# Loading the first quarter of W1 with two DMAs and two waits

## Chip, cores, metric

One NeuronCore of a Trainium2 chip. The metric is device microseconds of one execution, median of several. One execution in each set is profiled; times inside the profile are microseconds from the start of the span, which is about 1.7 us shorter than the device time. Engines: PE is TensorE (PEld its weight loads), DVE VectorE, ACT ScalarE, POOL GpSimd, SP SyncE; ACTq and SPq are their sequencers, which issue DMAs.

## The reference

```python
# x: (1, 2048, 640) bf16; w1: (640, 1536); w2: (1536, 640); wqkv: (640, 1920); wo: (640, 640)
xn = _layernorm(x)
return x + linear_attention(xn, wqkv, wo) + (gelu(xn @ w1 + b1) @ w2 + b2)
```

All that matters here is the first product, `xn @ w1`: it can start when the first 128 rows of x are normalised and transposed, and the first columns of W1 are in SBUF.

## The kernel before

A small planner records instructions for each engine and puts a semaphore wait on an instruction for every resource (`r_...`) that it reads or writes and that another engine or a DMA last wrote. Each DMA has a semaphore of its own. W1 lies in SBUF as `W1[p, k, f]`, row `128*k + p`, and is loaded in four quarters of 384 columns. The loads, in order of issue on each engine:

```python
        FW = F // NW1
        def dma_w1(i, eng="sync"):
            dma_w(eng, W1[:, :, i * FW:(i + 1) * FW], w1v[:, :, i * FW:(i + 1) * FW], r_W1[i])
        dma_x(0, 1)
        dma_w("scalar", b1tmp[:], B_b1.rearrange("(a p) -> a p", p=P), r_b1tmp)
        dma_w1(0, "scalar")
        dma_x(1, 1)
        dma_w1(1)
        dma_x(2, 1)
        dma_w1(2)
        # ... x tile 3, quarter 3, the rest of x, all on SyncE
```

I call the quarters 0 to 3 in code "quarter 1" to "quarter 4" in the text; the change touches quarter 1. The first three blocks of hidden units, for the first 128 rows of x, are computed in two parts, since the transposed x tile 0 comes in two pieces:

```python
        def h_first(jbs):
            bs = [take(1) for _ in jbs]
            for (ks, res) in (((0, 1), r_xnTA), ((2, 3, 4), r_xnT[0])):
                for jb, b in zip(jbs, bs):
                    Pl.ins("tensor", [(lambda e, k=k, jb=jb, b=b: e.matmul(
                        bank(b, 0, P), W1[:, k, jb * P:(jb + 1) * P], xnT[:, k, 0:P],
                        start=(k == 0), stop=(k == DT - 1))) for k in ks],
                        reads=[r_W1[jb * P // FW], res], writes=[B_[b]])
        # ... then one GELU for each block on ScalarE

        filler(10)                         # matmuls on zeros, to raise TensorE's clock
        ln_stats(0)                        # layer norm statistics of x tile 0
        ln_half(1, 0); ln_half(1, 1); ln_aggr(1)
        norm0(0, CA, r_xnA)                # columns 0 to 255 of x tile 0
        norm0(CA, D, r_xnB)                # the rest
        dA, sA, bA = transp0(0, 2, r_xnA)  # TensorE
        filler(1)
        dB, sB, bB = transp0(2, DT, r_xnB)
        # VectorE copies the first piece to xnT (r_xnTA), ScalarE the second (r_xnT[0])
        # ...
        b1_step()                          # transposes b1 on TensorE
        ln_norm(1)
        h_first([0, 1, 2])
```

The "first part" below is 6 matmuls over rows 0 to 255 of W1, the "second part" 9 matmuls over the other 384.

## Time and profile before

| | before |
|---|---|
| device time, median of 3 (range) | 210.89 us (210.71 to 210.95) |
| span of the profiled execution | 209.0 us |
| TensorE busy | 204.9 us, 98% |
| share of TensorE in the chain that ended last | 92% |
| second part of the first units starts | 7.38 us |

The page of the kernel before, its busy line and its chain of work that ended last:

```profile
PE 204.9 (98%) x1599; PEld 141.0 (67%) x1599; DVE 108.8 (52%) x227; ACT 75.1 (36%) x142; POOL 20.2 (10%) x61
...
PE 92%; DVE 6%; issue 1%; DVEq 0%
```

TensorE is the bound. From 7.4 to 60 us the start times of its matmuls show no pause over 0.03 us. So a microsecond that TensorE loses before 7.4 us is lost in the total, and the place to look is the first 8 us. The timeline there, before (start, duration, engine, line, operation, out<-in, count; in brackets the idle time before it and what ended that; in all these cuts "..." or a jump in time stands for lines left out):

```profile
0.80 0.63 ACTq L234 DMA_DIRECT2D b1tmp<-in_B_b_dram  x1
0.81 0.87 SPq L230 DMA_DIRECT2D xPK<-in_A_x_dram  x2
1.46 0.41 ACTq L234 DMA_DIRECT2D W<-in_B_w_dram  x1
1.73 0.43 SPq L234 DMA_DIRECT2D W<-in_B_w_dram  x1
...
6.72 0.09 PEld L303 LDWEIGHTS ps<-ident,b1tmp 12*128 12x128 bf16 x1
...
6.83 0.49 ACT L408 ACTIVATE xnT<-ps 128x384 bf16<-128x384 bf16 x1 [3.44 <-PE ps L375]
6.84 1.22 PE L385 MATMUL ps<-xnT,W 128*128 128x128 bf16 x15
...
7.38 0.51 PEld L385 LDWEIGHTS ps<-xnT,W 128*128 128x128 bf16 x9 [0.20 <-ACT xnT L408]
```

L385 is `h_first`. Its first 6 matmuls start at 6.84, when the transpose of b1 has left TensorE; the other 9 at 7.38, released by ScalarE's copy (L408), which ran from 6.83 to 7.32. The DMA issues, before (size, median time from issue to landing):

```profile
W<-in_B_w_dram SPq DMA_DIRECT2D x3, 480.0 KB, 7.0
W<-in_B_w_dram ACTq DMA_DIRECT2D x1, 480.0 KB, 5.2
```

Quarter 1, issued by ScalarE at 1.46, lands 5.2 us later: each W1 DMA has sixteen completions in the trace, and the last of them, which I call its landing, is at 6.68. In this execution it does not hold TensorE.

### The profile page before, as it was taken

How to read it: one execution, taken by the hardware profiler on the slowest of the kernel's cores; microseconds unless marked ns; L12 is line 12 of the kernel's file. 1: busy time of each engine (PE TensorE's matmuls, PEld its weight loads, DVE VectorE, ACT ScalarE, POOL GpSimd, SP SyncE). 2: the span in 40 equal slices, each digit the busy share in tenths (PEclk: the TensorE clock that was granted, in tenths of full speed). 3: DMA queues.
4: the chain of work that ended last, by engine and by line, in shares of the span. 5: the costliest groups of instructions: out<-in, count | busy, mean ns of one | idle time of the engine just before them, and what ended most of it. 6: DMA issues, size and time to landing. Idle time of an engine off the chain costs nothing.

```text
span 209.0 us, 3950 instructions
## 1 busy us (share of the span) xinstructions
PE 204.9 (98%) x1599; PEld 141.0 (67%) x1599; DVE 108.8 (52%) x227; ACT 75.1 (36%) x142; POOL 20.2 (10%) x61
## 2 busy tenths in 40 slices
PE   7999999999999999999999999999999999999995
PEld 2799987444457777777756565577777777777775
DVE  4589970000008888999178975478633522523322
ACT  2689887666676444111253576100000000000000
POOL 3245568200000000000000000000000000000000
DMA  6999668997000000000000000591120111001001
GB/s 164 348 349 112 105 129 130 376 332 260 3 0 0 0 0 3 0 3 0 0 0 5 0 0 3 193 313 57 63 59 32 58 42 55 31 31 35 31 34 61
DMA packets 22507, 17.86 MB, mean 85 GB/s; under 512 B 9176, under 2 KB 22488, under 8 KB 22488
## 3 DMA queue, kind: packets, MB, share of 16 engines
q1 hardware_dynamic: 21808, 17.11, 29.1%
q10 hardware_dynamic: 680, 0.49, 0.9%
q8 instruction: 12, 0.20, 0.4%
q14 instruction: 7, 0.06, 0.1%
HBM read 12.62 MB, written 2.62 MB: 73 GB/s over the span
## 4 chain that ended last, share of the span: by engine, by line
PE 92%; DVE 6%; issue 1%; DVEq 0%
PE ps L617 33%; PE ps L355 25%; PE ps L487 10%; PE ps L476 10%; PE ps L509 5%; DVE PQ L466 3%; PE ps L298 2%; PE ps L653 2%; DVE ek L464 1%; DVE W L533 1%; PE ps L529 1%; PE ps L545 1%; DVE ZB L523 1%; PE ps L555 1%; PE ps L385 1%
## 5 line engine op out<-in xcount | busy, mean ns | idle before, releaser
L355 PE MATMUL ps<-xnT,W 128*128 128x128 bf16 (+2 forms) x435 | 52.0, 282 | 0.0
L617 PE MATMUL ps<-W,HG 128*128 128x320 bf16 x360 | 51.4, 299 | 0.0
L355 PEld LDWEIGHTS ps<-xnT,W 128*128 128x128 bf16 x435 | 35.6, 98 | 15.6
L617 PEld LDWEIGHTS ps<-W,HG 128*128 128x128 bf16 x360 | 35.1, 98 | 14.2 <-issue 0.4
L359 ACT ACTIVATE HG<-ps,b1c 128x128 bf16<-128x128 f32 (+2 forms) x87 | 40.1, 493 | 12.4 <-PE ps L355 10.3
L464 DVE TENSOR_SCALAR ek<-ek 128x512 bf16<-128x512 bf16 (+1 forms) x36 | 11.0, 305 | 42.7 <-ACT ek L463 41.6
L636 DVE TENSOR_TENSOR out_sb<-ps,xnT 128x640 bf16<-128x640 f32 x15 | 12.4, 825 | 36.2 <-PE ps L617 36.1
L463 ACT ACTIVATE ek<-ps 128x512 bf16<-128x512 f32 (+1 forms) x36 | 23.2, 645 | 20.4 <-PE ps L509 11.2
L617 PE MATMUL ps<-Msb,PQ 128*128 128x320 bf16 x150 | 22.5, 299 | 0.0
L509 PE MATMUL ps<-xnT,Wqkv 128*128 128x512 bf16 x100 | 22.1, 379 | 0.0
L476 PE MATMUL ps<-Wqkv,xnT 128*128 128x320 bf16 x160 | 21.9, 299 | 0.0
L487 PE MATMUL ps<-xPK,xn_tm 128*128 128x320 bf16 x160 | 21.9, 299 | 0.0
L476 PEld LDWEIGHTS ps<-Wqkv,xnT 128*128 128x128 bf16 x160 | 15.7, 98 | 6.2
L487 PEld LDWEIGHTS ps<-xPK,xn_tm 128*128 128x128 bf16 x160 | 15.7, 98 | 6.1
L617 PEld LDWEIGHTS ps<-Msb,PQ 128*128 128x128 bf16 x150 | 14.6, 98 | 5.7
L509 PEld LDWEIGHTS ps<-xnT,Wqkv 128*128 128x128 bf16 x100 | 11.6, 117 | 9.6 <-issue 0.2
L466 DVE SCALAR_TENSOR_TENSOR PQ<-ps,ek 128x512 bf16<-128x512 f32 x20 | 13.8, 692 | 2.1
L311 DVE BATCH_NORM_STATS2 stats<-xPK 128x6 f32<-128x320 bf16 x32 | 13.6, 466 | 2.3 <-DMA xPK<-in_A_x_dram 2.3
L466 DVE SCALAR_TENSOR_TENSOR xPK<-ps,ek 128x640 bf16<-128x640 f32 x16 | 13.2, 824 | 1.7
L497 DVE TENSOR_TENSOR Msb<-Msb,xPK 128x640 f32<-128x640 f32 x14 | 11.6, 825 | 0.5
L491 ACT ACTIVATE W<-ps 128x640 bf16<-128x640 f32 x5 | 3.5, 704 | 18.2 <-PE ps L487 14.6
L321 POOL TENSOR_TENSOR rstd<-aggr,mhalf 128x1 f32<-128x1 f32 x16 | 9.1, 568 | 8.9 <-DVE aggr L319 8.9
(68 smaller groups left out, 93.7 us busy)
## 6 DMA issues: line engine op xcount, KB each, us to landing
xnT<-in_A_x_dram SPq DMA_DIRECT2D x4, 640.0 KB, 6.2
Wqkv<-in_A_wqkv_dram SPq DMA_DIRECT2D x3, 800.0 KB, 6.7
out_dram<-out_sb SPq DMA_DIRECT2D x15, 160.0 KB, 1.8
W<-in_B_w_dram SPq DMA_DIRECT2D x1, 1920.0 KB, 15.3
W<-in_B_w_dram SPq DMA_DIRECT2D x3, 480.0 KB, 7.0
xPK<-in_A_x_dram SPq DMA_DIRECT2D x2, 640.0 KB, 9.5
Wo<-in_A_wo_dram SPq DMA_DIRECT2D x1, 800.0 KB, 10.5
xPK<-in_A_x_dram SPq DMA_DIRECT2D x4, 160.0 KB, 4.2
```

Of the source, the lines that this page charges most:

```text
L311: Pl.ins(v, lambda e: e.bn_stats(stats[:, s, 6 * h:6 * h + 6], x_in[:, t, h * HW:(h + 1) * HW]), reads=[r_x[t]], writes=[r_stats[s][h]])
L355: Pl.ins("tensor", [(lambda e, k=k: e.matmul(bank(b, 0, w), W1[:, k, jb * P:(jb + 1) * P], xnT[:, k, tok], start=(k == 0), stop=(k == DT - ...
L359: Pl.ins("scalar", lambda e: e.activation(HG[:, jb, tok], bank(b, 0, w), ACT.Gelu_apprx_tanh, bias=b1c[:, jb:jb + 1]), reads=[B_[b], r_b1c ...
L463: Pl.ins("scalar", lambda e: e.activation(e2, src, ACT.Exp), reads=br, writes=[r_ek[s]])
L464: Pl.ins(v, lambda e: e.tensor_scalar(et, et, 1.0, 1e-6, ALU.min, ALU.add), reads=[r_ek[s]], writes=[r_ek[s]])
L466: Pl.ins(v, lambda e: e.scalar_tensor_tensor(out=d2, in0=src, scalar=0.0, in1=e2, op0=ALU.max, op1=ALU.add), reads=br + [r_ek[s]], writes= ...
L476: fns.append(lambda e, k=k, h=h, b=b, t=t: e.matmul(bank(b + h, 0, HW), xnT[:, k, t * P:(t + 1) * P], Wqkv[:, k, D + h * HW:D + (h + 1) * ...
L487: Pl.ins("tensor", [(lambda e, t=t, h=h, b=b, f=f: e.matmul(bank(b + h, 0, HW), xn_tm[:, t, f * P:(f + 1) * P], PK[:, t, h * HW:(h + 1) * ...
L497: Pl.ins(v, lambda e, t=t: e.tensor_tensor(out=zsum, in0=zsum, in1=PK[:, t, :], op=ALU.add), reads=[r_PK[t], r_zsum], writes=[r_zsum])
L509: Pl.ins("tensor", [(lambda e, k=k, j=j, b=b: e.matmul(bank(b), Wqkv[:, k, j:D:DT], xnT[:, k, cc], start=(k == 0), stop=(k == DT - 1))) fo ...
L617: return lambda e: e.matmul(bank(b + h, 0, HW), l, r[:, h * HW:(h + 1) * HW], start=(i == 0), stop=(i == JT + DT - 1))
L636: Pl.ins(v, lambda e: e.tensor_tensor(out=halves(out_sb[:, s, :]), in0=pair(b), in1=halves(x_res[:, t, :]), op=ALU.add), reads=B_[b:b + 2] ...
```

## The change

The intent: rows 0 to 255 are all that the first part reads, so load them with a DMA of their own, and let the first part start without the other 384 rows.

```diff
+        r_W1a = R_("W1_0a")
@@
-        dma_w1(0, "scalar")
+        dma_w("scalar", W1[:, 0:2, 0:FW], w1v[:, 0:2, 0:FW], r_W1a)
+        dma_w("scalar", W1[:, 2:DT, 0:FW], w1v[:, 2:DT, 0:FW], r_W1[0])
@@ def h_first
-                        reads=[r_W1[jb * P // FW], res], writes=[B_[b]])
+                        reads=[r_W1a if res is r_xnTA else r_W1[0], res], writes=[B_[b]])
```

The order of instructions on TensorE, VectorE, GpSimd and SyncE is unchanged; ScalarE issues one DMA more.

## The prediction

> **What bounds it now.** TensorE: busy 98% of the 209.0 us span, 92% of the chain that ended last, granted clock 1.00. From 7.4 to 60 us I find no pause of TensorE over 0.03 us in the trace's start times, so what delays TensorE before 7.4 us passes into the total almost one to one.
>
> **The first microseconds (timeline, DMA issues with time to landing).** ScalarE issues b1 (0.80, taking 0.63) and the first W1 quarter at 1.46, taking 0.41; SyncE issues x tiles 0 and 1 (0.81, 1.25), then W1 quarter 2 at 1.73. Quarter 1 lands 5.2 us after issue: 6.68. Quarter 2 lands at 7.82. TensorE ends the transposes of x tile 0, does the b1 transpose at 6.73, and starts the first part of the first units (6 matmuls, rows 0 to 255) at 6.84. Its other operand was copied by 6.45, and the b1 transpose holds TensorE until about 6.83. So quarter 1 arrives some 0.15 us before it can matter. The second part (9 matmuls) starts at 7.38, released by ScalarE's copy (6.83 to 7.32), not by W1: the chain of waits names that copy, 0.20 us idle.
>
> **What the change does.** No engine instruction is added or reordered; ScalarE gets one more DMA issue (0.41 us, early; its next needed work is at 6.83). First-part matmuls wait for 192 KB, second-part ones for the other 288 KB.
> - Gain: rows 0 to 255 land earlier, an estimate of 5 to 6 us. The first part still cannot start before the b1 transpose is done, 6.8. Worth 0 to 0.1 us (up to 0.2 if in unprofiled runs quarter 1 lands later).
> - Cost: the second DMA is issued when the first's issue is over, about 1.9 us, 0.17 us *after* SyncE's quarter 2. The landings here follow the order of issue across both issuers: 6.68 (quarter 1), 7.82 (quarter 2, 480 KB, +1.14), 8.30 (x tile 2, 160 KB, +0.49), 9.79 (quarter 3, +1.49). Quarter 1 on ScalarE's queue did not share with SyncE's quarter 2 as equals, or it would not land 1.14 us ahead. The Trainium skill (DMA: Bandwidth & Descriptors, "Issuing engines are not separate DMA queues") says they share 16 engines whoever issues; its "Queues, rings and completion order" has round robin between queues. This trace looks more like order of issue. So I expect the 288 KB behind quarter 2: the bytes up to there are those of before up to quarter 2, landing about 7.8 (7.5 if they alternate). The second part then starts at about 7.85 in place of 7.38: +0.45 us, and TensorE has no later slack.
>
> **Time.** 210.89 + 0.45 x about 0.7 (the chance that order of issue holds): 211.2 us; 210.75 to 211.6 in 8 of 10. Faster by 2%: 0.01; within: 0.97; slower: 0.02.
>
> **What would show it.** Timeline: first part at 6.8 as before; first matmul of the second part at 7.8, released by a W1 DMA, not by the copy. DMA issues: the first piece lands about 4 us after issue, the second about 5.9.
>
> **What would make it wrong.** ScalarE's second piece served ahead of quarter 2 (its queue preferred, or the issue shorter): landing about 6.7, time equal, perhaps 0.1 us less. Quarter 1 arriving late in ordinary executions: then a small gain. A shift of x tile landings or of the clock's warming (fillers run at 0.43 us each, half rate, until about 6.8).

## The result

| | before | after |
|---|---|---|
| device time, median of 6 (range) | 210.87 us (210.71 to 211.03) | 211.44 us (211.03 to 212.19) |
| ratio, 95% interval | | 1.0030 (1.0013 to 1.0047) |
| span of the profiled execution | 209.0 us | 209.7 us |
| first part starts | 6.84 us | 6.57 us |
| second part starts | 7.38 us | 8.12 us |

A ratio is the mean time of one kernel's fast runs over that of the other's of the same rounds, so not quite the ratio of the medians. A run more than 1.5% above the fastest of its kernel is marked slow, and is in no ratio. The loss is 0.3%, far inside the 2% that would be called slower, but it is resolved.

The page of the kernel after, the same two lines:

```profile
PE 204.0 (97%) x1599; PEld 140.6 (67%) x1599; DVE 108.7 (52%) x227; ACT 75.0 (36%) x142; POOL 20.1 (10%) x61
...
PE 89%; DVE 6%; DMA 3%; issue 1%; ACTq 0%; DVEq 0%
```

A DMA now has 3% of the chain; there was none. The timeline after, the lines that answer to those of before:

```profile
1.46 0.92 ACTq L235 DMA_DIRECT2D W<-in_B_w_dram  x2
...
1.72 0.43 SPq L235 DMA_DIRECT2D W<-in_B_w_dram  x1
...
6.56 0.49 ACT L410 ACTIVATE xnT<-ps 128x384 bf16<-128x384 bf16 x1 [2.66 <-PE ps L377]
...
6.57 0.51 PE L387 MATMUL ps<-xnT,W 128*128 128x128 bf16 x6
...
8.12 0.50 PEld L387 LDWEIGHTS ps<-xnT,W 128*128 128x128 bf16 x9 [1.22 <-DMA W<-in_B_w_dram]
```

ScalarE's copy (L410) was done at 7.05; the second part still starts only at 8.12, released by a W1 DMA. The DMA issues after:

```profile
W<-in_B_w_dram SPq DMA_DIRECT2D x3, 480.0 KB, 7.4
...
W<-in_B_w_dram ACTq DMA_DIRECT2D x1, 288.0 KB, 6.2
W<-in_B_w_dram ACTq DMA_DIRECT2D x1, 192.0 KB, 3.2
```

The 192 KB for the first part land at 4.62, two microseconds before anything can use them. The 288 KB, issued at 1.89, land at 8.08: 1.40 us later than the whole 480 KB did before.

The first part's earlier start (6.57 against 6.84) is not the work of the change. In this execution TensorE came to full rate at about 4.5 us (the fillers' starts are 0.43 us apart until then, and about half of that afterwards), in the first profile of before only at about 6.8 (all its fillers are at half rate, and from 6.34 to 6.56 the transposes of x tile 0 still start 0.11 us apart, in place of 0.06 to 0.07 here). The second profiles of both kernels show about 6.1. The Trainium skill says this of the clock ("TensorE: Matmul & The Clock Gate", "Part 1: The HAM clock gate"): the window that decides is free-running, so the point of warming varies from run to run. The traces here agree that it varies, and by more than the ±500 ns that the section names: from about 4.1 us (e1) to almost 7 us (e7), with the same order of instructions on TensorE.

Why so late? The DMA packets of the changed kernel between 5 and 6 us, by queue (q1 is SyncE's, q10 ScalarE's; packets, MB, share of 16 engines' time):

```profile
q1 hardware_dynamic: 202, 0.15, 50.3%
q10 hardware_dynamic: 196, 0.15, 46.0%
```

Between 4 and 5 us it had been:

```profile
q1 hardware_dynamic: 273, 0.21, 80.1%
q10 hardware_dynamic: 95, 0.07, 20.5%
```

First quarter 2, which SyncE issued 0.17 us ahead of ScalarE's second piece, has most of the engines; then the two queues share them about equally, and both transfers end late (the second piece at 8.08, quarter 2 at 8.30). In r_after, the second profile of this kernel, the counts are 244 to 48 between 4 and 5 us, 218 to 152 between 5 and 6, and 208 to 172 between 6 and 7: a lead and then turns, but not packet for packet. In before the lead was on the other side, with quarter 1, between 4 and 5 us:

```profile
q10 hardware_dynamic: 270, 0.20, 66.6%
q1 hardware_dynamic: 93, 0.07, 24.1%
```

The Trainium skill ("DMA: Bandwidth & Descriptors", "Queues, rings and completion order") says that each DMA engine goes round robin between the queues that it has work for; 202 to 196 packets agrees, 218 to 152 only roughly.

Turns are not the whole of it. Twelve of the second piece's sixteen completions were in by 6.79, before ScalarE's copy was done at 7.05; the other four came at 7.19, 7.44, 7.56 and 8.08 (in r_after eleven by 7.09, five from 7.71 to 8.65). The second part waited for these few. Why they lag, no run here shows.

### The profile page after: what moved, and what is told of

It reads as the page before. It is cut to its first block, busy times and chain, and to the rows that moved or that the text cites. A ratio compares the mean times of both kernels' runs of the same rounds, so it can differ in the third digit from the quotient of the medians.

```text
span 209.7 us, 3952 instructions
## 1 busy us (share of the span) xinstructions
PE 204.0 (97%) x1599; PEld 140.6 (67%) x1599; DVE 108.7 (52%) x227; ACT 75.0 (36%) x142; POOL 20.1 (10%) x61
## 4 chain that ended last, share of the span: by engine, by line
PE 89%; DVE 6%; DMA 3%; issue 1%; ACTq 0%; DVEq 0%
PE ps L619 33%; PE ps L357 25%; PE ps L478 10%; PE ps L489 10%; PE ps L511 5%; DVE PQ L468 3%; DMA W<-in_B_w_dram 3%; PE ps L655 2%; DVE ek L466 1%; DVE W L535 1%; PE ps L531 1%; PE ps L547 1%; DVE ZB L525 1%; PE ps L557 1%; ACTq L235 0%
```

## The experiments

Theory ORDER, from the prediction: the second piece is late because it is issued behind quarter 2. Its rival SPLIT: two DMAs cost this by being two. Later the theory had to be sharpened. The first four ran on one chip, the next four on another, the last four on the first chip again; the versions on one chip share its runs of the kernel before (first chip 210.51 to 211.46 and one run at 213.06 with a mean clock of 0.992; second chip 210.53 to 211.22). Five rounds each. All results were correct.

### e1_second_first: the second piece on SyncE, ahead of quarter 2

```diff
         dma_w("scalar", W1[:, 0:2, 0:FW], w1v[:, 0:2, 0:FW], r_W1a)
-        dma_w("scalar", W1[:, 2:DT, 0:FW], w1v[:, 2:DT, 0:FW], r_W1[0])
         dma_x(1, 1)
+        dma_w("sync", W1[:, 2:DT, 0:FW], w1v[:, 2:DT, 0:FW], r_W1[0])
         dma_w1(1)
```

> The split stays, both waits stay; only the second piece's issue moves from ScalarE's queue (1.89 us, behind W1 quarter 2 at 1.72) to SyncE's queue, between x tile 1 and quarter 2. Theory ORDER (the second piece is late because quarter 2 was issued before it, and the two queues then share the DMA engines): it lands at about 6.7 to 7.2 us, the second part of the first units starts at 7.1 to 7.4 released by ScalarE's copy, time 210.9 us (ratio to the kernel before 0.998 to 1.001), spread narrow again. Rival SPLIT (two DMAs in place of one cost 0.6 us by themselves: an additional issue, more completions, smaller pieces): it still lands at about 8 us, time about 211.4.

Measured: 210.47 us (210.42 to 210.63), ratio 0.9972 (0.9937 to 1.0006; the width comes from the run of before at 213.06). The piece was issued at 1.73 and landed at 6.21; the second part started at 7.15. SPLIT falls: the same two DMAs and two waits, with the second DMA ahead of quarter 2 on SyncE's queue, cost nothing. The time is even below the 210.9 that ORDER gave.

### e2_q2_later: both pieces on ScalarE, quarter 2 after x tile 2

```diff
-        dma_w1(1)
         dma_x(2, 1)
+        dma_w1(1)
```

> Both pieces stay on ScalarE's queue; quarter 2 is issued on SyncE only after x tile 2, so the second piece is issued ahead of it. ORDER: second piece at about 6.8 to 7.3 us, second part of the first units at 7.2 to 7.5; quarter 2 lands at about 8.3, close to its first use at 8.2, so up to 0.2 us may be lost there: time 210.8 to 211.1. SPLIT, or a rival in which ScalarE's second issue in a row is what is slow: second piece at about 8 us, time about 211.4.

Measured: 211.09 us (210.70 to 211.36), ratio 0.9998 (0.9966 to 1.0030). The second piece, now issued 0.29 us ahead of quarter 2, landed at 7.63, later than ORDER's 6.8 to 7.3. So its second part started earlier than that of the change (7.68 against 8.12), but being issued ahead of quarter 2 was not enough: between 5 and 6 us this kernel's ScalarE queue moved 152 packets beside SyncE's 307.

### e3_whole_late: no split, quarter 1 issued behind quarter 2

```diff
 # on the kernel before
         dma_w("scalar", b1tmp[:], B_b1.rearrange("(a p) -> a p", p=P), r_b1tmp)
+        dma_w("scalar", b1dup[:], B_b1.rearrange("(a p) -> a p", p=P), r_b1dup)
         dma_w1(0, "scalar")
```

(`b1_step` waits for `b1dup` too, so that something waits for that DMA.)

> The kernel before, not split, one wait; a second 3 KB load of b1 is put ahead of quarter 1 on ScalarE's queue, so that the whole quarter 1 is issued at about 2.1 us, behind quarter 2 (1.72 us). ORDER: it lands at about 8.0 to 8.5 us, both parts of the first units wait for it, the second begins at about 8.4 to 8.8 in place of 7.38: time 211.8 to 212.4 with no split at all. SPLIT: an issue 0.65 us later costs at most that much of landing, about 7.3 us, and the second part starts at about 7.7: time at most 211.2.

Measured: 214.23 us (211.90 to 215.72), ratio 1.0129 (1.0078 to 1.0179). The additional issue took only 0.30 us, so quarter 1 was issued at 1.79, 0.06 us behind quarter 2 (1.73), and landed at 10.02. An unsplit quarter that is issued second is late too, which again speaks against SPLIT. But only one of the six runs had a mean clock of 1.000, 211.90 us, as expected; the others, at 0.992 and 0.984, paid for a halved TensorE clock (see e4). Runs at 0.992 still count as fast, since only the time decides; so the ratios of e3 and e4 mix two clocks, and I do not build on them. The profiled one is of the slow state, so I use its landing only as a sign, and not its time.

### e4_wait_both: the change's two DMAs, the first part waits for both

```diff
-                        reads=[r_W1a if res is r_xnTA else r_W1[0], res], writes=[B_[b]])
+                        reads=[r_W1a, r_W1[0], res], writes=[B_[b]])
```

> The changed kernel's two DMAs, but the first part of the first units waits for both pieces. It says what the split wait is worth when the second piece is late. If the second piece alone sets the pace, the 6 matmuls of the first part (0.34 us) move behind its landing: second part at about 8.45, time 0.34 us above the changed kernel, about 211.8. If something else released the second part, no difference: 211.4.

Measured: 213.92 us (211.66 to 215.51), ratio 1.0084 (1.0028 to 1.0139). The two runs with a mean clock of 1.000 took 211.66 and 212.04, about the 211.8 that was expected. The four others had 0.992 or 0.984. The profiled one is such a run; its TensorE by stretches (us, PE busy and count, granted clock, DMA share, GB/s):

```profile
5.00:7.00 2.00, 0.86 (x7) 1.00 1.02 330
7.00:8.00 1.00, 0.00 (x0) 0.76 1.04 355
8.00:9.00 1.00, 0.38 (x4) 0.50 1.08 365
9.00:14.00 5.00, 5.00 (x49) 0.50 1.08 353
```

TensorE waited from 6.9 to 8.6 for W1 (the second piece landed at 8.53), the clock fell to half in that wait, at about 7.5, and stayed there past 14 us. In the changed kernel the first part stands in the middle of that wait. TensorE's matmuls waited 1.05 and 1.52 us in its two profiled executions, at full clock; of its 12 timed runs one fell to 0.992 (214.41 us), here four of six. So the two full-clock runs fit the 0.34 us that the separate wait should be worth when the second piece is late, and the other four lost more. That it is the first part's 6 matmuls that save the clock is likely but was not isolated: the executions also differ in when the clock had come up (about 4.1 us here, 4.5 and 6.1 in the changed kernel).

### r_before and r_after: both kernels again, on the second chip

> The kernel before once more, for a second profile. In its first profile the fillers ran at half rate until about 6.8 us, while in all five profiles of kernels with a changed W1 load they did so only to about 4.5 us. If that is the chance of an execution, this profile can show either; where the clock rises at 4.5 us, TensorE reaches the first part at about 6.5 us and the unsplit quarter 1 (landing 6.3 to 7.2 us) holds it there: second part at landing + 0.4, or 7.1 us, whichever is later. If the change of W1 loading moves the clock itself, fillers are at half rate to about 6.8 us again. Time 210.8 to 210.95 in any case.

> The changed kernel again, in the same rounds as the others. Second piece between 7.6 and 8.5 us, alternating with W1 quarter 2; second part of the first units 0.05 us after it; time 211.3 to 211.6, spread wider than that of the kernel before, since a landing time is now on the chain.

Measured: r_before 210.78 us (210.71 to 211.10), ratio to before itself 1.0006 (0.9994 to 1.0018). r_after 211.42 us (211.13 to 214.41; the run at 214.41 is slow, and the five fast ones have a median of 211.22), ratio 1.0032 (1.0018 to 1.0046): the loss repeats. (The expectation of r_before says that in five profiles the fillers ran at half rate only to about 4.5 us; in e2 all ten did, to 5.5, so it was four of five.) The timeline of r_before:

```profile
6.50 0.18 PE L303 MATMUL ps<-ident,b1tmp 12*128 12x12 bf16 x1
7.07 1.01 PE L385 MATMUL ps<-xnT,W 128*128 128x128 bf16 x15 [0.39 <-DMA W<-in_B_w_dram]
```

Here TensorE was ready at 6.68 and did wait for quarter 1, which landed at 7.02. So the change aimed at a wait that exists in some executions of the kernel before. In r_after the second piece landed at 8.65, quarter 2 at 8.99, and the second part started at 8.70.

### e5_whole_q2_later: no split, quarter 2 after x tile 2

The edit of e2, on the kernel before.

> Not split, one wait: the kernel before, with W1 quarter 2 issued after x tile 2 in place of ahead of it. Theory SHARING (what counts is how much of quarter 2 is in the queues beside quarter 1; this is also why the version with the second piece ahead of quarter 2 beat the kernel before by 0.4 us): the whole quarter lands at about 6.0 to 6.5 us, time 210.5 to 210.7. Rival PIECES (that gain came from the two pieces and their separate waits): landing may be earlier but the time stays at 210.8 or above. Quarter 2 lands about 8.2 and is used at 8.0 to 8.2: up to 0.2 us may be lost to it.

Measured: 210.86 us (210.71 to 210.89), ratio 1.0004 (0.9992 to 1.0016). Quarter 1 landed at 6.90, no earlier. My SHARING was wrong as put: moving quarter 2 by one place left ScalarE's queue taking turns as before (199 packets beside SyncE's 228 between 5 and 6 us; x tile 2 and then quarter 2 stood there).

### e8_second_first_wait_both: e1, with the first part waiting for both pieces

The edit of e4, on e1.

> The faster version (second piece on SyncE ahead of quarter 2, 210.47 us), but its first part waits for both pieces. If the separate waits carry its gain, the first part must now wait for a second piece that comes after 6.5 us in many executions: 210.7 or more. If the gain is only that all of quarter 1 is in by about 6.2 us: 210.4 to 210.55, as with separate waits.

Measured: 210.97 us (210.31 to 212.07), ratio 1.0018 (0.9996 to 1.0040). In the profiled execution (210.40) the second piece landed at 5.50, long before TensorE was ready, and the double wait cost nothing. The other five spread over 1.8 us, against 0.2 us of e1 (0.4 in its second set). That fits executions in which a piece comes after 6.5 us, which separate waits would hide. The profile of e7 below, with the same loads, is one (6.95); but none of this kernel's own slower executions was profiled, and the chip was another one: open.

### e9_whole_sync: no split, quarter 1 on SyncE ahead of quarter 2

```diff
-        dma_w1(0, "scalar")
         dma_x(1, 1)
+        dma_w1(0)
         dma_w1(1)
```

> Not split, one wait, quarter 1 moved to SyncE's queue between x tile 1 and quarter 2 (issue about 1.72 us in place of 1.46). Theory RING (a transfer is slowed by whatever waits in the other queue, which is served alternately with it, and not by what stands behind it in its own; quarter 2 behind quarter 1 in one queue cannot take turns with it): the whole quarter lands at 5.4 to 6.4 us although it is issued 0.26 us later, its 16 completions within about 0.7 us, time 210.4 to 210.65, no split needed. Rival TWO QUEUES (quarter 1 came early in the version with the second piece on SyncE because its two pieces ran from two queues): landing 6.7 to 7.2 us, time 210.8 to 211.1.

Measured: 210.64 us as the median of five runs (210.44 to 210.82); a sixth took 1223.76 us, at a clock of 1.000, and is in no ratio; nothing in the profile of another run can explain it. Ratio 0.9979 (0.9940 to 1.0018), widened by the same run of before as in e1. The DMA issues of this kernel:

```profile
W<-in_B_w_dram SPq DMA_DIRECT2D x4, 480.0 KB, 6.0
```

Quarter 1, issued at 1.73 in place of 1.46, lands at 6.24 in place of 6.68 to 7.02, its sixteen completions within 1.0 us (5.23 to 6.24) in place of 1.8 to 2.0. And TensorE, released by ScalarE's copy again:

```profile
6.50 0.49 ACT L408 ACTIVATE xnT<-ps 128x384 bf16<-128x384 bf16 x1 [3.56 <-PE ps L375]
6.50 1.22 PE L385 MATMUL ps<-xnT,W 128*128 128x128 bf16 x15
...
7.04 0.51 PEld L385 LDWEIGHTS ps<-xnT,W 128*128 128x128 bf16 x9 [0.20 <-ACT xnT L408]
```

RING fits and TWO QUEUES (6.7 to 7.2) does not, in the one execution profiled: the same transfer, unsplit and issued later, comes earlier when quarter 2 stands behind it in its own queue and not beside it in another. A rival, that ScalarE's queue is simply served worse than SyncE's, was not tested by exchanging the two; against it, ScalarE's queue had the lead in before (270 packets to 93). The spread of 1.0 us is wider than the 0.7 I had expected.

### r_e1: e1 again

> The version with the second piece on SyncE ahead of quarter 2, again, since its first interval (0.9937 to 1.0006) was widened by one run of the kernel before at 213.06 us. 210.4 to 210.6 us, ratio 0.997 to 0.9985, clear of 1.

Measured: 210.48 us (210.36 to 210.78), ratio 0.9973 (0.9941 to 1.0005). The second piece landed at 5.78 and the second part started at 7.08. That is inside the range I gave, but the ratio's interval is not clear of 1 as I expected. Over both sets e1 has a median of 210.48 in 12 runs, 0.4 us under the kernel before. The interval still touches 1, because of the one run of before at 213.06, so by the interval the gain is not settled; the two spans (208.7 and 208.6 against 209.0 twice) agree with it.

### e6_norm_first and e7_norm_first_split: x tile 0 sooner

If all of quarter 1 is in by 6.2 us, x tile 0 binds. VectorE aggregates tile 1's statistics ahead of normalising tile 0; these two move that behind it.

```diff
         ln_half(1, 1)
-        ln_aggr(1)
         norm0(0, CA, r_xnA)
         norm0(CA, D, r_xnB)
+        ln_aggr(1)
```

> The kernel before (W1 loads unchanged) with VectorE normalising x tile 0 before it aggregates the statistics of tile 1: tile 0 reaches TensorE about 0.25 us earlier. If quarter 1's landing (6.68 and 7.02 us in the two profiles of before) already ends the wait of TensorE in most executions, little of it arrives: 210.65 to 210.85 us. If the chain of tile 0 is what binds, 210.55 to 210.65.

> The same reordering on top of the version with the second piece on SyncE, in which all of quarter 1 is in by 5.5 to 6.2 us. Tile 0's chain binds there, so the 0.25 us should arrive: second part of the first units at about 6.85 us, time 210.15 to 210.35.

Measured: e6 (on the kernel before) 211.16 us (210.40 to 211.32), ratio 0.9993 (0.9960 to 1.0027). Its profile shows what was expected, TensorE done with the b1 transpose at 6.4 and waiting for quarter 1 until 6.96; but the median is above the range I gave. e7 (on e1) 210.89 us (210.60 to 213.16), ratio 1.0007 (0.9959 to 1.0055), a miss. In its profile quarter 2 landed at 8.32 and now held the next units:

```profile
8.36 3.50 PEld L357 LDWEIGHTS ps<-xnT,W 128*128 128x128 bf16 x55 [0.26 <-DMA W<-in_B_w_dram]
8.37 3.78 PE L357 MATMUL ps<-xnT,W 128*128 128x128 bf16 x55
```

TensorE had begun the last matmul before that at 8.06. Also TensorE was at half rate until almost 7 us there, so the second part began at 7.33 instead of 6.85. And the second piece, loaded as in e1, landed at 6.95: fifteen of its completions were in by 5.52, one came 1.4 us later. A place in SyncE's queue ahead of quarter 2 does not keep off such a late one. One gain uncovers the next wait; neither version is better than e1.

### One number for all of them

The span of the profiled execution less the start of the second part:

| kernel | second part starts | span | difference |
|---|---|---|---|
| before, r_before | 7.38, 7.42 | 208.96, 208.98 | 201.58, 201.56 |
| after, r_after | 8.12, 8.70 | 209.67, 210.25 | 201.55, 201.55 |
| e1, r_e1 | 7.15, 7.08 | 208.71, 208.62 | 201.56, 201.54 |
| e2 | 7.68 | 209.28 | 201.60 |
| e5 | 7.44 | 209.13 | 201.69 |
| e8 | 7.03 | 208.68 | 201.65 |
| e9 | 7.04 | 208.80 | 201.76 |
| e6 | 7.31 | 208.88 | 201.57 |
| e7 (held again by quarter 2) | 7.33 | 209.25 | 201.92 |

The starts differ by 1.67 us, the differences by 0.22 without e7. So the whole effect of each of these versions is in when the second part starts. (e3 and e4 are left out: their profiled executions ran at half clock.)

## Why the prediction was right

- **Where the time can go.** "What delays TensorE before 7.4 us passes into the total almost one to one": held, by the table above.
- **The second part is delayed and a W1 DMA releases it.** Held: 8.12 and 8.70 in place of about 7.4.
- **The size.** I expected the second piece at about 7.8 and +0.45 us. It landed at 8.08 and 8.65, +0.74 and +1.3 us in the two profiled executions; in the medians of the fast runs the loss was 0.57 and 0.37 (211.44 less 210.87, 211.22 less 210.85). I had discounted 0.45 to 0.3 by a 0.7 chance; the forecast 211.2 was 0.24 low, inside the range. That it fell inside is partly luck: the 0.45 us belonged to strict order of issue, which did not hold (the second piece landed ahead of quarter 2); for taking turns I had 7.5, and the 0.58 us from there to 8.08 came with the few late completions, which I had not foreseen.
- **The mechanism, half right.** "This trace looks more like order of issue" does not hold as a rule. The queues did take turns (202 to 196 packets); order of issue decides only who has a head start. What I read as strict order before, quarter 1 landing 1.14 us ahead of quarter 2, was a lead (270 packets to 93 between 4 and 5 us) after a head start of 0.27 us of issue, and then turns: between 5 and 6 us before, ScalarE's queue still moved 142 packets beside SyncE's 288. e2 and e5 showed that the place in the issue order is not enough, while with a place ahead of quarter 2 in quarter 2's own queue (e1 twice, e8, e9, e7) it landed at 5.5 to 6.24 in four of five profiles and at 6.95 in one. Why it came still later than my 7.5 for turns is not settled: four of the sixteen completions lag (the first came at 6.34, the twelfth at 6.79, the last at 8.08), and which engine or why the traces do not say.
- **The gain.** "Quarter 1 arrives some 0.15 us before it can matter ... worth 0 to 0.1 us (up to 0.2 ...)": true of the one execution that I had. r_before waited 0.39 us for it (e6 0.55), so the wait that the change aimed at is real. Even so its worth is bounded by ScalarE's copy, before which the second part cannot start. In r_before the copy was done at 7.10 and the second part started at 7.42, behind the first part that had waited: up to about 0.27 us to win there (an estimate, with the 0.05 us that lie between copy and matmul in e9), had the other rows come in time. That r_before and before have the same span within 0.02 us is chance: one was held by W1 and the other by the half-rate clock.

## What to carry to other kernels

When a transfer that TensorE waits for is split, look at what is issued between the pieces: the second piece here went behind and then alternately with 480 KB from the other queue, and came 1.4 us later than the unsplit transfer (1.6 in the second pair of profiles), its last few completions above all. Put an urgent transfer in the same queue ahead of the bulk that follows it, rather than in a second queue beside it; then the split is hardly needed (e9 without it 210.64 us, e1 with it 210.48; neither gain over the kernel before is clear of noise). And read the wait at the start of a kernel from more than one profile: from execution to execution the landing moved by tenths of a microsecond, sometimes by more than one, and the warming of the clock by almost three.

## What the Trainium skill lacked or had wrong

- "DMA: Bandwidth & Descriptors", "Queues, rings and completion order": the round robin agrees with 202 to 196 packets (in r_after, 218 to 152, only roughly). It lacks that a transfer issued 0.17 us later in the other queue starts well behind: between 4 and 5 us its queue had 95 packets (some of them still the first piece's) to the other's 273.
- The same page, "Issuing engines are not separate DMA queues" and the row on spreading DMAs in "Rules for kernel authors", say that spreading DMAs over issuing engines only saves issue time (the row says it of bandwidth). For the landing of one urgent transfer the choice mattered here: the same 480 KB, from ScalarE at 1.46 landed at 6.68 and 7.02, from SyncE at 1.73 at 6.24 (one profile).
- "TensorE: Matmul & The Clock Gate", "Why this matters for your kernels": it warns of gaps over about 3 us between bursts of matmuls. In e4 the clock fell at about 7.5 us, 0.6 us into a wait that began at 6.9; the pauses of TensorE around it were 1.05 us (until 6.04) and 1.72 us. That two shorter pauses can do it too is what the warning lacks; between 5 and 7 us TensorE was busy for 0.86 us, most of it transposes, so this one execution does not show the 3 us to be wrong.
- No page that I read has this: the profile's granted clock reads 1.00 in the first microseconds while the fillers' starts are 0.43 us apart; in these first microseconds the rate has to be read from the spacing of matmuls.
